# K loaded in rows of 16 KB with one batch and head per DMA engine, w2 in five chunks, the output stored in four transfers on two queues

## The chip, the cores and the metric

One core of a Trainium2 chip. The metric is the time of one execution on the device in microseconds (us), the median of several runs. A profile's span is some 1.8 us shorter than the time of the same run, because it begins with the first instruction and ends with the last; differences between spans and differences between times can be compared.

## The reference, cut to what matters

Four tokens (batch 4, one position each) go through a modulated layer norm, attention over cached keys and values, an output projection, a second layer norm and a feed-forward network with a ReLU.

```python
mod = (silu(c) @ w_mod)                       # six modulation vectors
h = layernorm(x) * (1 + ca) + sa
q = (h @ wq)                                  # 32 query heads of 128
k, v = k_cache[:, :, -1024:, :], v_cache[...] # 4 batches x 8 heads x 1024 keys x 128, bf16
o = softmax(q k^T / sqrt(128)) v
x = x + ga * (o @ wo)
h = layernorm(x) * (1 + cb) + sb
out = x + gb * (relu(h @ w1) @ w2)
```

K and V are 8 MB each, wq and wo 4 MB each, w_mod 3 MB, w1 and w2 1.8 MB each: 32 MB come in, 4 KB go out. Each of the 32 (batch, head) pairs has its 256 KB of K in one piece; two pairs start 1 MiB apart, because the cache holds 4,096 keys of which the last 1,024 are used.

## The kernel before

K comes in eight tiles of 1 MB, each half of the heads of one batch. A partition gets one row of 8 KB (32 keys). The order is "position, then head": 32 groups of four partitions, one partition for each of four heads.

```python
    def load_k(gi):
        b, par = gi // 2, gi % 2
        kt_ = kvpool.tile([P, NI, Dh], bf16, tag="kv", name=f"k{gi}")
        nc.sync.dma_start(
            out=kt_[:].rearrange("p j d -> p (j d)"),
            in_=k_src[b, par, :, S - W:, :].rearrange("h (p j) d -> p h (j d)", j=NI),
        )
        k_tiles.append(kt_)
```

TensorE transposes each tile in 32 blocks, VectorE and ScalarE move the result from PSUM to SBUF, and TensorE multiplies it with the queries. Softmax, the product with V, wo, w1 and w2 follow. All loads stand in one queue, issued by SyncE, in this order: K0, K1, w_mod, wq, K2 to K7, V, wo, w1, w2. w2 comes in chunks of 6, 5, 2 and 1 rows per partition so that little is left to do after the last; the result goes out in one transfer of 16 rows of 256 bytes:

```python
    W2_CHUNKS = [(0, 6), (6, 5), (11, 2), (13, 1)]
    ...
    nc.sync.dma_start(out=out.rearrange("b o (g n) -> (o g) b n", g=NH), in_=res[::BS, :])
```

Of the kernel before, what the change touches and what calls it, by code (L numbers as in the profile page):

```python
# [8 lines left out]
ACT = mybir.ActivationFunctionType  # L9
ALU = mybir.AluOpType  # L10
AX = mybir.AxisListType
bf16 = mybir.dt.bfloat16
f32 = mybir.dt.float32
i32 = mybir.dt.int32
# [3 lines left out]
def kernel(  # L18
# [14 lines left out]
    nc = tc.nc  # L33
    P = 128
    B, Sq, D = A_x.shape
    _, Hkv, S, Dh = A_k_cache.shape
    Hq = A_wq.shape[1] // Dh
    rep = Hq // Hkv
    W = min(4096, max(256, S // 4))
    Dff = B_w1.shape[1]  # L40
    DT = D // P
    FT = Dff // P
    KT = W // P
    assert Dh == P and B * Hq == P and Sq == 1
    CG = 32
    assert Hkv * rep == CG and B == 4 and rep == 4 and Hkv == 8 and DT == 4 and D == 512
    scale = float(Dh) ** -0.5
    EPS = 1e-5
    HALF = W // 2
    NHW = Hkv // 2  # L50
    NG = 2 * B
    KC = P // NHW
    NI = W // KC
    KAHEAD = 2
    NH = 4
    DH2 = D // NH
    BS = CG // B
# [3 lines left out]
    const = ctx.enter_context(tc.tile_pool(name="const", bufs=1))  # L61
    wts = ctx.enter_context(tc.tile_pool(name="wts", bufs=1))
    kvpool = ctx.enter_context(tc.tile_pool(name="kvpool", bufs=11))
    ktp = ctx.enter_context(tc.tile_pool(name="ktp", bufs=4))
    work = ctx.enter_context(tc.tile_pool(name="work", bufs=1))
    psA = ctx.enter_context(tc.tile_pool(name="psA", bufs=6, space=bass.MemoryType.PSUM))
# [7 lines left out]

    k_src = A_k_cache.rearrange("b (par hw) s d -> b par hw s d", par=2)
    k_tiles = []

    def load_k(gi):
        b, par = gi // 2, gi % 2
        kt_ = kvpool.tile([P, NI, Dh], bf16, tag="kv", name=f"k{gi}")  # L80
        nc.sync.dma_start(  # L81
            out=kt_[:].rearrange("p j d -> p (j d)"),
            in_=k_src[b, par, :, S - W:, :].rearrange("h (p j) d -> p h (j d)", j=NI),
        )
        k_tiles.append(kt_)

    for gi in range(KAHEAD):
        load_k(gi)
    wmod_sb = wts.tile([P, DT, 6 * D], bf16, tag="med", name="wmod_sb")
# [3 lines left out]
    for t in range(0, DT, 2):  # L93
        nc.sync.dma_start(out=wq_sb[:, t:t + 2, :], in_=wq_src[:, t:t + 2, :])
    for gi in range(KAHEAD, NG):
        load_k(gi)

    v_tiles = []
    for h in range(Hkv):
        vt_ = kvpool.tile([P, NI, Dh], bf16, tag="kv", name=f"v{h}")  # L100
        nc.sync.dma_start(
            out=vt_[:].rearrange("p j d -> p (j d)"),
            in_=A_v_cache[:, h, S - W:, :].rearrange("b (p j) d -> p b (j d)", j=NI),
        )
        v_tiles.append(vt_)
# [14 lines left out]

    W2_CHUNKS = [(0, 6), (6, 5), (11, 2), (13, 1)]
    assert sum(e for _, e in W2_CHUNKS) == FT
    w2_dst = w12[:, DT * Dff:DT * Dff + FT * D]
    for (m0, e) in W2_CHUNKS:
        nc.sync.dma_start(out=w2_dst[:, m0 * D:(m0 + e) * D],
                          in_=B_w2[m0 * P:(m0 + e) * P, :].rearrange("(q e) n -> q (e n)", e=e))
# [3 lines left out]
    ident_bf = const.tile([P, P], bf16, name="ident_bf")  # L130
    make_identity(nc, ident_bf[:])

    ident_k3 = const.tile([P, NHW, KC], bf16, name="ident_k")
    nc.gpsimd.memset(ident_k3[:], 0.0)
    nc.gpsimd.affine_select(out=ident_k3[:], in_=ident_k3[:], compare_op=ALU.not_equal, fill=1.0, base=0,
                            pattern=[[-1, NHW], [-NHW, KC]], channel_multiplier=1)
    ident_k = ident_k3[:].rearrange("p h k -> p (h k)")

# [17 lines left out]
                            base=0, pattern=[[-1, NL], [0, 2], [-NL, P // NL]], channel_multiplier=1)  # L156
# [19 lines left out]
    for t in range(DT):  # L176
# [8 lines left out]
                                   op0=ALU.is_ge, op1=ALU.max)  # L185
# [8 lines left out]
    sc_ps = psS.tile([P, W], f32, tag="s", name="sc_ps")  # L194
    IQ = NI // 4

    def k_transposes(gi):
        kT = ktp.tile([P, NI, NHW, KC], bf16, tag="kT", name=f"kT{gi}")
        for iq in range(4):
            tp = psA.tile([P, IQ, P], bf16, tag="t", name=f"ktp_{gi}_{iq}")  # L200
            for ii in range(IQ):
                nc.tensor.transpose(out=tp[:, ii, :], in_=k_tiles[gi][:, iq * IQ + ii, :], identity=ident_k)  # L202
            dst = kT[:, iq * IQ:(iq + 1) * IQ].rearrange("p i h k -> p i (h k)")
            if iq % 2 == 1:
                nc.vector.tensor_copy(out=dst, in_=tp[:])  # L205
            else:
                nc.scalar.copy(out=dst, in_=tp[:])  # L207
        return kT

    def k_scores(gi, kT):  # L210
        b, par = gi // 2, gi % 2
        for half in range(2):
            for hw in range(NHW):
                nc.tensor.matmul(  # L214
                    out=sc_ps[hw * CG:(hw + 1) * CG, half * HALF:(half + 1) * HALF],
                    lhsT=qpad[:, b, par, hw, :],
                    rhs=kT[:, half * (NI // 2):(half + 1) * (NI // 2), hw, :],
                    start=(gi == 0), stop=(gi == NG - 1),
                    tile_position=(0, hw * CG),
                )  # L220

    kts_pending = [k_transposes(gi) for gi in range(KAHEAD)]


    m4 = const.tile([P, B], f32, name="m4")
    nc.vector.tensor_reduce(out=m4[:], in_=ident_f[:].rearrange("p (hp b r) -> p b hp r", b=B, r=rep),
                            axis=AX.XY, op=ALU.add)
# [10 lines left out]
    for t in range(DT):  # L238
        nc.tensor.matmul(out=m5_ps[:], lhsT=siluT32[:, t, :], rhs=wmod_sb[:, t, 4 * D:5 * D],  # L239
                         start=(t == 0), stop=(t == DT - 1), tile_position=(0, 0))  # L240
# [68 lines left out]

    for gi in range(KAHEAD):  # L310
        k_scores(gi, kts_pending.pop(0))
    kts_pending.append(k_transposes(KAHEAD))
    for gi in range(KAHEAD, NG):
        if gi + 1 < NG:
            kts_pending.append(k_transposes(gi + 1))
        k_scores(gi, kts_pending.pop(0))



    mx = work.tile([P, 1], f32, name="mx")  # L320
    nc.vector.tensor_reduce(out=mx[:], in_=sc_ps[:], axis=AX.X, op=ALU.max)
    nb = work.tile([P, 1], f32, name="nb")
    nc.vector.tensor_scalar_mul(out=nb[:], in0=mx[:], scalar1=-scale)
    NQ = 4
# [4 lines left out]
    den4 = work.tile([P, NQ], f32, name="den4")  # L329
    p_rep = ktp.tile([P, NI // 2, P, 2], bf16, tag="kT", name="p_rep")  # L330
    p_w = p_rep[:].rearrange("q u c e -> q (u c e)").bitcast(i32).rearrange("q (w b) -> q w b", b=B)
    pT = ktp.tile([P, NI, P], bf16, tag="kT", name="pT")
    oT_ps = psA.tile([P, NHW, 2, B, rep], f32, tag="t", name="oT_ps")
# [9 lines left out]
    VEARLY = 3  # L343
    for iq in range(NQ):
        ws = slice(iq * WQ, (iq + 1) * WQ)
        nc.scalar.activation(out=e_sb[:, ws].rearrange("q (u k e) -> q u k e", k=KC, e=2),  # L346
                             in_=sc_ps[:, ws].rearrange("q (u e k) -> q u k e", e=2, k=KC), func=ACT.Exp,
                             bias=nb[:], scale=scale, accum_out=den4[:, iq:iq + 1])
    for iq in range(NQ):
# [123 lines left out]

    for (m0, m1) in [(0, 6), (6, FT)]:
        ffn1(m0, m1)
# [6 lines left out]
    nc.vector.tensor_tensor(out=res[:], in0=zg[:], in1=x12_ps[:], op=ALU.add)  # L482
    nc.sync.dma_start(out=out.rearrange("b o (g n) -> (o g) b n", g=NH), in_=res[::BS, :])

# [29 lines left out]
```

## Time and profile before

| | before |
|---|---|
| time, median (lowest to highest) | 85.94 us (85.81 to 85.98, 3 runs) |
| span of the profile | 84.1 us |
| bytes in | 31.99 MB |
| DMA engines busy | from 2 us to 80 us without a gap |
| TensorE busy | 57.5 us (68% of the span) |

Packet times in this document are medians over the trace's records of single DMA packets, and sums of them are what was recorded for all 16 engines, divided by 16. The kernel is bound by its loads, as the lines in the prediction show. Of the costliest groups of instructions one line is wanted later. Its columns: line, engine, operation, what is written and read, shapes, count; then busy us and mean ns of one; then idle time of the engine just before, and what ended it.

```profile
L202 PE MATMUL ktp<-ident_k,k 128*128 128x128 bf16 x256 | 18.4, 241 | 1.2 <-DMA k<-in_A_k_cache_dram 1.2
```

In the whole K stage TensorE waited only 1.2 us for K.

### The profile page before, as it was taken

What the parts mean: (1) busy time and instruction counts of PE and PEld (TensorE: products, weight loads), DVE (VectorE), ACT (ScalarE), POOL (GpSimd) and SP (SyncE); (2) the same over time, 40 slices, a digit from 0 to 9 for tenths busy, and PEclk for the clock granted to TensorE, in tenths of its full rate; (3) what the DMA queues carried; (4) which work ended last, traced back from release to release, by engine and by line L of the source; (5) the groups of instructions that cost most, each with busy time, mean ns of one, the idle gap of its engine ahead of it and who ended that gap; (6) DMA issues with size and microseconds to landing.
All of it is one profiled execution on the core that took longest, in us unless ns stands there. A gap on an engine that the chain in (4) does not pass through costs nothing.

```text
span 84.1 us, 2367 instructions
## 1 busy us (share of the span) xinstructions
PE 57.5 (68%) x1064; PEld 47.4 (56%) x1064; DVE 26.4 (31%) x73; ACT 23.5 (28%) x37; POOL 5.2 (6%) x20
## 2 busy tenths in 40 slices
PE   0029940499729899999999329996454478598840
PEld 0029940248629739977778029996452058588720
DVE  0144480030330103645665768500003020241420
ACT  2314670003020004977798196300000010001000
POOL 6980000000000000000000000000000000000000
PEclk9999999957955555999999995696555555555555
DMA  0999998999999999999999999999999999999500
GB/s 2 333 401 452 503 421 386 444 421 444 421 394 405 433 433 413 413 413 425 425 413 409 425 425 421 405 433 421 425 409 409 425 432 425 413 398 406 210 0 2
DMA packets 4077, 32.13 MB, mean 382 GB/s; under 512 B 476, under 2 KB 612, under 8 KB 996
## 3 DMA queue, kind: packets, MB, share of 16 engines
q1 hardware_dynamic: 4052, 31.99, 91.7%
q8 instruction: 8, 0.13, 0.6%
q10 hardware_dynamic: 16, 0.01, 0.0%
q14 instruction: 1, 0.01, 0.0%
HBM read 31.99 MB, written 0.00 MB: 381 GB/s over the span
## 4 chain that ended last, share of the span: by engine, by line
DMA 64%; PE 25%; DVE 3%; issue 2%; SPq 1%; ACT 1%; DVEq 0%
DMA w<-in_B_w_dram 24%; DMA v<-in_A_v_cache_dram 24%; DMA wmod_sb<-in_w_mod_dram 16%; PE ktp L202 9%; PE qT_ps L302 4%; PE sc_ps L214 4%; PE mT L253 2%; PE mT L255 2%; PE z_ps L470 2%; PE m_ps L236 2%; SPq L81 1%; PE m_ps L239 1%; PE gb_ps L244 1%; PE st_ps_var L269 1%; ACT lnv L286 0%
## 5 line engine op out<-in xcount | busy, mean ns | idle before, releaser
L202 PEld LDWEIGHTS <-k 128*128 128x128 bf16 x256 | 17.3, 110 | 3.9 <-issue 2.5
L202 PE MATMUL ktp<-ident_k,k 128*128 128x128 bf16 x256 | 18.4, 241 | 1.2 <-DMA k<-in_A_k_cache_dram 1.2
L207 ACT COPY kT<-ktp 128x1024 bf16<-128x1024 bf16 x16 | 15.5, 1016 | 13.2 <-PE ktp L202 12.1
L205 DVE COPY kT<-ktp 128x1024 bf16<-128x1024 bf16 x16 | 11.1, 691 | 11.6 <-PE ktp L202 11.3
L340 PE MATMUL oT_ps<-pT,v 128*128 128x16 bf16 x256 | 7.3, 172 | 2.5 <-issue 1.9
L340 PEld LDWEIGHTS <-v 128*128 128x128 bf16 x256 | 7.1, 100 | 2.7 <-issue 2.0
L214 PE MATMUL sc_ps<-kT,qpad 128*32 128x512 bf16 x64 | 5.6, 445 | 0.4 <-DVE qpad L306 0.4
L357 PE MATMUL pT_ps<-ident_bf,p_rep 128*128 128x128 bf16 x32 | 3.1, 278 | 2.9 <-DVE p_rep L351 2.9
L357 PEld LDWEIGHTS <-p_rep 128*128 128x128 bf16 x32 | 2.7, 127 | 3.4 <-DVE p_rep L351 3.4
L302 PE MATMUL qT_ps<-hT,wq_sb 128*128 128x4 bf16 x128 | 3.6, 166 | 1.4 <-DVE ab L295 1.4
L302 PEld LDWEIGHTS <-wq_sb 128*128 128x128 bf16 x128 | 3.5, 104 | 1.5 <-issue 1.5
L236 PE MATMUL m_ps<-wmod_sb,siluT 128*32 128x512 bf16 x16 | 1.3, 435 | 4.4 <-DMA wmod_sb<-in_w_mod_dram 4.4
L409 ACT COPY y<-y_ps 128x256 f32<-128x256 f32 x1 | 0.4, 372 | 11.4 <-DVE y L408 11.4
L404 PE MATMUL y_ps<-wo_sb,o 128*32 128x512 bf16 x16 | 2.1, 619 | 2.0 <-DMA wo_sb<-in_A_wo_dram 1.1
L177 PE MATMUL tp<-ident_bf,cx_sb 8*128 8x8 bf16 x4 | 0.3, 168 | 4.5 <-DMA cx_sb<-in_A_x_dram 4.5
L236 PEld LDWEIGHTS <-siluT 128*32 128x32 bf16 x16 | 0.4, 95 | 4.7 <-issue 4.5
L382 DVE TENSOR_TENSOR oT_sb<-oT_ps,rb 128x128 bf16<-128x128 f32 x1 | 0.3, 292 | 8.6 <-PE oT_ps L340 8.6
L416 PEld LDWEIGHTS <-wo_sb 128*128 128x128 bf16 x64 | 2.5, 121 | 0.6 <-DMA wo_sb<-in_A_wo_dram 0.6
L416 PE MATMUL y_ps<-o,wo_sb 128*128 128x4 bf16 x64 | 2.4, 173 | 0.5 <-DMA wo_sb<-in_A_wo_dram 0.5
L177 PEld LDWEIGHTS <-cx_sb 8*128 8x128 bf16 x4 | 0.2, 110 | 4.5 <-issue 4.5
L351 DVE TENSOR_TENSOR p_rep<-e_sb,mi 128x512 int32<-128x512 int32 x4 | 2.5, 685 | 0.7 <-ACT e_sb L346 0.7
L459 PE MATMUL u_ps<-ab,w 128*128 128x8 bf16 x56 | 2.4, 181 | 0.4 <-DMA w<-in_B_w_dram 0.4
(107 smaller groups left out, 57.0 us busy)
## 6 DMA issues: line engine op xcount, KB each, us to landing
k<-in_A_k_cache_dram SPq DMA_DIRECT2D x8, 1024.0 KB, 25.8
v<-in_A_v_cache_dram SPq DMA_DIRECT2D x8, 1024.0 KB, 19.9
wq_sb<-in_A_wq_dram SPq DMA_DIRECT2D x2, 2048.0 KB, 18.0
wo_sb<-in_A_wo_dram SPq DMA_DIRECT2D x4, 1024.0 KB, 19.9
wmod_sb<-in_w_mod_dram SPq DMA_DIRECT2D x1, 3072.0 KB, 13.7
w<-in_B_w_dram SPq DMA_DIRECT2D x1, 1792.0 KB, 21.7
w<-in_B_w_dram SPq DMA_DIRECT2D x1, 768.0 KB
w<-in_B_w_dram SPq DMA_DIRECT2D x1, 640.0 KB, 20.1
```

Of the source, the lines that this page charges most:

```text
L202: nc.tensor.transpose(out=tp[:, ii, :], in_=k_tiles[gi][:, iq * IQ + ii, :], identity=ident_k)
L205: nc.vector.tensor_copy(out=dst, in_=tp[:])
L207: nc.scalar.copy(out=dst, in_=tp[:])
L214: nc.tensor.matmul(out=sc_ps[hw * CG:(hw + 1) * CG, half * HALF:(half + 1) * HALF], lhsT=qpad[:, b, par, hw, :], rhs=kT[:, half * (NI // 2 ...
L236: nc.tensor.matmul(out=m4_ps[k * CG:(k + 1) * CG, :], lhsT=siluT32[:, t, :], rhs=wmod_sb[:, t, k * D:(k + 1) * D], start=(t == 0), stop=(t ...
L302: nc.tensor.matmul(out=qT_v[:, hq, :], lhsT=wq_sb[:, t, hq * Dh:(hq + 1) * Dh], rhs=hT[:, t, :], start=(t == 0 and hq == 0), stop=(t == DT ...
L340: nc.tensor.matmul(out=oT_ps[:, hw, par].rearrange("p b r -> p (b r)"), lhsT=v_tiles[h][:, i, :], rhs=pT[:, i, c0:c0 + B * rep], start=(fi ...
L351: nc.vector.tensor_tensor(out=p_w[:, ws, :], in0=e_w[:, ws].unsqueeze(2).to_broadcast([P, WQ // 2, B]), in1=mi4[:].unsqueeze(1).to_broadca ...
L357: nc.tensor.transpose(out=tp[:, ii, :], in_=p_rep[:, i // 2, :, i % 2], identity=ident_bf[:])
L404: nc.tensor.matmul(out=y4_ps[q0:q0 + CG, :], lhsT=o4[:, l, g % 2, g // 2, :], rhs=wo_sb[:, g, l, :], start=(g == 0 and l < 4), stop=(g == ...
L416: nc.tensor.matmul(out=y_ps[:, m, :], lhsT=wo_sb[:, g, l, m::DT], rhs=o4[:, l, g % 2, g // 2, 0:B], start=False, stop=(g == NP - 1 and l = ...
L459: nc.tensor.matmul(out=u_ps[:, m - m0].rearrange("p s b -> p (s b)"), lhsT=w1_cols(t, m), rhs=ab[:, t].rearrange("p s b -> p (s b)"), star ...
```

## The change

Three things at once. K comes in 2 MB tiles: each partition gets 16 KB (64 keys) instead of 8, and the order is "pair of batch and head, then position", so that 16 groups of 8 partitions arise, meant to give each of the 16 DMA engines one pair and one piece of 128 KB in HBM. w2 comes in five chunks. The store is cut in four, two on each of two queues.

```diff
-    k_src = A_k_cache.rearrange("b (par hw) s d -> b par hw s d", par=2)
+    k_src = A_k_cache.rearrange("b h s d -> (b h) s d")
...
+    def load_k(ti, parts):
+        bh, kh = ti // 2, ti % 2
+        kt_ = kvpool.tile([P, NI8, Dh], bf16, tag="kv", name=f"k{ti}")
+        e = NI8 // parts
+        s0 = S - W + kh * WH
+        src = k_src[bh * NQK:(bh + 1) * NQK, s0:s0 + WH, :].rearrange("q (k j) d -> q k (j d)", j=NI8)
+        for i0 in range(0, NI8, e):
+            nc.sync.dma_start(out=kt_[:, i0:i0 + e, :].rearrange("p j d -> p (j d)"), in_=src[:, :, i0 * Dh:(i0 + e) * Dh])
...
-    W2_CHUNKS = [(0, 6), (6, 5), (11, 2), (13, 1)]
+    W2_CHUNKS = [(0, 4), (4, 4), (8, 3), (11, 2), (13, 1)]
...
-    for (m0, m1) in [(0, 6), (6, FT)]:
+    for (m0, m1) in [(0, 8), (8, FT)]:
...
-    nc.sync.dma_start(out=out.rearrange("b o (g n) -> (o g) b n", g=NH), in_=res[::BS, :])
+    out_g = out.rearrange("b o (g n) -> g (b o) n", g=NH)
+    for g in range(NH):
+        eng = nc.sync if g % 2 == 0 else nc.scalar
+        eng.dma_start(out=out_g[g], in_=res[g * CG:(g + 1) * CG:BS, :])
```

Cut away: the K and V buffers become five of 16 KB per partition instead of eleven of 8 KB; transposes, score matmuls and exponentials follow the new order of keys; the maximum before the exponential is taken in two halves. The source of a K transfer, as it stands in the program, has these dimensions (elements of 2 bytes; step and count, slowest first):

```
before   [4096, 32] [524288, 4] [1, 4096]     32 groups of 4 partitions
changed  [524288, 16] [8192, 8] [1, 8192]     16 groups of 8 partitions
```

More of the change, by code (lines that the diff above doesn't have):

```diff
@@ L50 @@
     NHW = Hkv // 2
-    NG = 2 * B
     KC = P // NHW
     NI = W // KC
-    KAHEAD = 2
+    NQK = 16
+    KC8 = P // NQK
+    NI8 = 2 * NI
+    WH = KC8 * NI8
+    NT = B * Hkv * W // (NQK * WH)
+    assert NQK == 2 * Hkv and WH == HALF and NT == 4
     NH = 4
@@ L62 @@
     wts = ctx.enter_context(tc.tile_pool(name="wts", bufs=1))
-    kvpool = ctx.enter_context(tc.tile_pool(name="kvpool", bufs=11))
-    ktp = ctx.enter_context(tc.tile_pool(name="ktp", bufs=4))
+    kvpool = ctx.enter_context(tc.tile_pool(name="kvpool", bufs=5))
+    ktp = ctx.enter_context(tc.tile_pool(name="ktp", bufs=2))
     work = ctx.enter_context(tc.tile_pool(name="work", bufs=1))
@@ L72 @@
     nc.scalar.dma_start(out=cx_sb[B:2 * B, :], in_=A_x.rearrange("b o d -> (b o) d"))
-    k_src = A_k_cache.rearrange("b (par hw) s d -> b par hw s d", par=2)
+    k_src = A_k_cache.rearrange("b h s d -> (b h) s d")
     k_tiles = []
-    def load_k(gi):
-        b, par = gi // 2, gi % 2
-        kt_ = kvpool.tile([P, NI, Dh], bf16, tag="kv", name=f"k{gi}")
-        nc.sync.dma_start(
-            out=kt_[:].rearrange("p j d -> p (j d)"),
-            in_=k_src[b, par, :, S - W:, :].rearrange("h (p j) d -> p h (j d)", j=NI),
-        )
+    def load_k(ti, parts):
[6 more added lines that the diff above has]
+            nc.sync.dma_start(out=kt_[:, i0:i0 + e, :].rearrange("p j d -> p (j d)"), in_=src[:, :, i0 * Dh:(i0 + e) * Dh])
         k_tiles.append(kt_)
-    for gi in range(KAHEAD):
-        load_k(gi)
+    load_k(0, 1)
     wmod_sb = wts.tile([P, DT, 6 * D], bf16, tag="med", name="wmod_sb")
@@ L94 @@
         nc.sync.dma_start(out=wq_sb[:, t:t + 2, :], in_=wq_src[:, t:t + 2, :])
-    for gi in range(KAHEAD, NG):
-        load_k(gi)
+    for ti in range(1, NT):
+        load_k(ti, 1 if ti + 1 < NT else 2)
     v_tiles = []
     for h in range(Hkv):
-        vt_ = kvpool.tile([P, NI, Dh], bf16, tag="kv", name=f"v{h}")
+        if h % 2 == 0:
+            v2_ = kvpool.tile([P, 2, NI, Dh], bf16, tag="kv", name=f"v{h}")
+        vt_ = v2_[:, h % 2]
         nc.sync.dma_start(
-            out=vt_[:].rearrange("p j d -> p (j d)"),
+            out=vt_.rearrange("p j d -> p (j d)"),
             in_=A_v_cache[:, h, S - W:, :].rearrange("b (p j) d -> p b (j d)", j=NI),
@@ L131 @@
     make_identity(nc, ident_bf[:])
-    ident_k3 = const.tile([P, NHW, KC], bf16, name="ident_k")
-    nc.gpsimd.memset(ident_k3[:], 0.0)
-    nc.gpsimd.affine_select(out=ident_k3[:], in_=ident_k3[:], compare_op=ALU.not_equal, fill=1.0, base=0,
-                            pattern=[[-1, NHW], [-NHW, KC]], channel_multiplier=1)
-    ident_k = ident_k3[:].rearrange("p h k -> p (h k)")
     siluT32 = const.tile([P, DT, CG], bf16, name="siluT32")
@@ L195, with k_transposes, k_scores @@
     IQ = NI // 4
-    def k_transposes(gi):
-        kT = ktp.tile([P, NI, NHW, KC], bf16, tag="kT", name=f"kT{gi}")
+    kTs = {}
+    def k_transposes(ti, sh):
+        if sh == 0:
+            kTs[ti] = ktp.tile([P, NI8, P], bf16, tag="kT", name=f"kT{ti}")
         for iq in range(4):
-            tp = psA.tile([P, IQ, P], bf16, tag="t", name=f"ktp_{gi}_{iq}")
+            tp = psA.tile([P, IQ, P], bf16, tag="t", name=f"ktp_{ti}_{sh}_{iq}")
+            i0 = sh * NI + iq * IQ
             for ii in range(IQ):
-                nc.tensor.transpose(out=tp[:, ii, :], in_=k_tiles[gi][:, iq * IQ + ii, :], identity=ident_k)
-            dst = kT[:, iq * IQ:(iq + 1) * IQ].rearrange("p i h k -> p i (h k)")
+                nc.tensor.transpose(out=tp[:, ii, :], in_=k_tiles[ti][:, i0 + ii, :], identity=ident_bf[:])
             if iq % 2 == 1:
-                nc.vector.tensor_copy(out=dst, in_=tp[:])
+                nc.vector.tensor_copy(out=kTs[ti][:, i0:i0 + IQ, :], in_=tp[:])
             else:
-                nc.scalar.copy(out=dst, in_=tp[:])
-        return kT
-    def k_scores(gi, kT):
-        b, par = gi // 2, gi % 2
-        for half in range(2):
-            for hw in range(NHW):
+                nc.scalar.copy(out=kTs[ti][:, i0:i0 + IQ, :], in_=tp[:])
+    def k_scores(ti, i0=0, i1=NI8):
+        bh, kh = ti // 2, ti % 2
+        for bl in range(2):
+            for h in range(Hkv):
+                b, par, hw = 2 * bh + bl, h // NHW, h % NHW
+                p0 = bl * (P // 2) + h * KC8
                 nc.tensor.matmul(
-                    out=sc_ps[hw * CG:(hw + 1) * CG, half * HALF:(half + 1) * HALF],
+                    out=sc_ps[hw * CG:(hw + 1) * CG, kh * WH + i0 * KC8:kh * WH + i1 * KC8],
                     lhsT=qpad[:, b, par, hw, :],
-                    rhs=kT[:, half * (NI // 2):(half + 1) * (NI // 2), hw, :],
-                    start=(gi == 0), stop=(gi == NG - 1),
+                    rhs=kTs[ti][:, i0:i1, p0:p0 + KC8],
+                    start=(b == 0 and par == 0), stop=(b == B - 1 and par == 1 and i1 == NI8),
                     tile_position=(0, hw * CG),
                 )
-    kts_pending = [k_transposes(gi) for gi in range(KAHEAD)]
+    for sh in range(2):
+        k_transposes(0, sh)
     m4 = const.tile([P, B], f32, name="m4")
@@ L308 @@
             in_=qT_ps[:, par].rearrange("p h r b -> p b h r"))
-    for gi in range(KAHEAD):
-        k_scores(gi, kts_pending.pop(0))
-    kts_pending.append(k_transposes(KAHEAD))
-    for gi in range(KAHEAD, NG):
-        if gi + 1 < NG:
-            kts_pending.append(k_transposes(gi + 1))
-        k_scores(gi, kts_pending.pop(0))
-    mx = work.tile([P, 1], f32, name="mx")
-    nc.vector.tensor_reduce(out=mx[:], in_=sc_ps[:], axis=AX.X, op=ALU.max)
+    k_scores(0)
+    for sh in range(2):
+        k_transposes(1, sh)
+    k_transposes(2, 0)
+    k_scores(1)
+    k_transposes(2, 1)
+    k_transposes(3, 0)
+    k_scores(2)
+    mx2 = work.tile([P, 2], f32, name="mx2")
+    nc.vector.tensor_reduce(out=mx2[:, 0:1], in_=sc_ps[:, 0:WH], axis=AX.X, op=ALU.max)
+    k_transposes(3, 1)
+    k_scores(3, 0, NI)
+    k_scores(3, NI, NI8)
+    nc.vector.tensor_reduce(out=mx2[:, 1:2], in_=sc_ps[:, WH:W], axis=AX.X, op=ALU.max)
     nb = work.tile([P, 1], f32, name="nb")
-    nc.vector.tensor_scalar_mul(out=nb[:], in0=mx[:], scalar1=-scale)
+    nc.vector.tensor_scalar(out=nb[:], in0=mx2[:, 0:1], scalar1=mx2[:, 1:2], scalar2=-scale, op0=ALU.max, op1=ALU.mult)
     NQ = 4
@@ L329 @@
     den4 = work.tile([P, NQ], f32, name="den4")
-    p_rep = ktp.tile([P, NI // 2, P, 2], bf16, tag="kT", name="p_rep")
-    p_w = p_rep[:].rearrange("q u c e -> q (u c e)").bitcast(i32).rearrange("q (w b) -> q w b", b=B)
-    pT = ktp.tile([P, NI, P], bf16, tag="kT", name="pT")
+    p_full = ktp.tile([P, NI8, P], bf16, tag="kT", name="p_full")
+    p_rep = p_full[:, 0:NI, :].rearrange("q n c -> q (n c)").rearrange("q (u c e) -> q u c e", c=P, e=2)
+    p_w = p_rep.rearrange("q u c e -> q (u c e)").bitcast(i32).rearrange("q (w b) -> q w b", b=B)
+    pT = ktp.tile([P, NI8, P], bf16, tag="kT", name="pT")
     oT_ps = psA.tile([P, NHW, 2, B, rep], f32, tag="t", name="oT_ps")
@@ L343 @@
     VEARLY = 3
-    for iq in range(NQ):
-        ws = slice(iq * WQ, (iq + 1) * WQ)
-        nc.scalar.activation(out=e_sb[:, ws].rearrange("q (u k e) -> q u k e", k=KC, e=2),
-                             in_=sc_ps[:, ws].rearrange("q (u e k) -> q u k e", e=2, k=KC), func=ACT.Exp,
-                             bias=nb[:], scale=scale, accum_out=den4[:, iq:iq + 1])
+    e_v = e_sb[:].rearrange("q (u a k s e) -> q a s u k e", a=2, k=KC8, s=2, e=2)
+    for kh in range(2):
+        for sh in range(2):
+            c0 = kh * WH + sh * NI * KC8
+            nc.scalar.activation(out=e_v[:, kh, sh],
+                                 in_=sc_ps[:, c0:c0 + NI * KC8].rearrange("q (u e k) -> q u k e", e=2, k=KC8), func=ACT.Exp,
+                                 bias=nb[:], scale=scale, accum_out=den4[:, 2 * kh + sh:2 * kh + sh + 1])
     for iq in range(NQ):
```

## The prediction

> **What bounds the kernel now.** I read the strip of the span first, then the chain that ended last, then the tail of the timeline. The strip says whether any stage leaves the DMA engines idle:
>
> ```profile
> DMA  0999998999999999999999999999999999999500
> GB/s 2 333 401 452 503 421 386 444 421 444 421 394 405 433 433 413 413 413 425 425 413 409 425 425 421 405 433 421 425 409 409 425 432 425 413 398 406 210 0 2
> ...
> q1 hardware_dynamic: 4052, 31.99, 91.7%
> ```
>
> The first row is the busy share in tenths of the 16 DMA engines in 40 slices of 2.1 us, the second what they moved, the third the load queue: packets, MB, share of the 16 engines' span. From slice 1 to slice 36 the engines are full. 31.99 MB has to come in, and nothing leaves the chip but 4 KB. The chain of waits says the same in time:
>
> ```profile
> 31.13 4.91 PE ktp L202 x64
> ...
> 39.39 19.88 DMA v<-in_A_v_cache_dram
> 59.28 20.14 DMA w<-in_B_w_dram
> 79.42 0.04 issue
> 79.46 1.31 PE z_ps L470 x30
> 80.79 0.30 DVE zg L480
> 81.12 0.29 DVE res L482
> ```
>
> Columns: start, length (us), what. TensorE is on the chain only up to 39 us, and only because a transfer issued then stands 20 us deep in a queue that is full anyway. From there to 79.4 it is V, then the weights. That TensorE is not the limit later shows in where it waits for V:
>
> ```profile
> 60.06 1.07 PE L340 MATMUL oT_ps<-pT,v 128*128 128x16 bf16 x34 [1.87 <-issue]
> ...
> 61.77 1.02 PE L340 MATMUL oT_ps<-pT,v 128*128 128x16 bf16 x32 [0.63 <-DMA v<-in_A_v_cache_dram]
> ...
> 66.73 1.05 PE L404 MATMUL y_ps<-wo_sb,o 128*32 128x512 bf16 x8 [1.15 <-DMA wo_sb<-in_A_wo_dram]
> ...
> 81.44 0.69 SPq L483 DMA_DIRECT2D out_dram<-res  x1
> ```
>
> The brackets are idle time before the group. TensorE stands idle 1.87 + 0.63 = 2.5 us just before the last V tile, so everything earlier in the K stage and the softmax has about 2.5 us of slack before it could move the end.
>
> Three numbers come from the trace's records of single packets and completions. **Packets:** on the load queue, medians are 312 ns for 8,192 bytes, 611 for 16,384, 199 for 5,120, 236 for 6,144, 84 for 2,048, 46 for 1,024, with hardly any spread (the 90th percentile of the 8,192-byte ones is 319). A DMA engine therefore works at its own rate, and the row length counts: two 8,192-byte rows take 624 ns, one of 16,384 takes 611, so a row costs about 13 ns beyond its bytes. **Full engines:** each engine handles 8 rows of every load; 160 rows of 8 KB, 16 of 16 KB, 8 of 24 KB, 8 of 14 KB and the four chunks of w2 sum to 49.92 + 9.78 + 7.30 + 4.30 + 4.52 = 75.8 us, against 76.3 us from the first packet (2.18) to the first engine's finish (78.53). There is no gap to win. **The last engine:** the 16 completions of the last w2 chunk run from 78.53 to 80.41 us. About half of the engines lag, by up to 1.9 us, each after one of eight 16 KB packets on the instruction queue, which take 1.02 to 1.11 us and cost the engine that carries one some 1.1 to 1.5 us. The end is 80.41 plus a fixed tail: last four matmuls, two VectorE steps, store, closing barrier, to 84.08 (3.67 us).
>
> [...]
>
> **The change, part by part.**
>
> K rows. Before: 8 transfers, 64 rows of 8 KB per engine, 64 x 312 = 19.97 us. After: three transfers of 2 MB with 16 KB rows and a fourth in two halves of 8 KB rows, so per engine 24 x 611 + 16 x 312 = 19.66 us. Gain 0.31 us, on the path, as the engines are full.
>
> w2 in five chunks of 4, 4, 3, 2, 1 rows instead of 6, 5, 2, 1. A row of 4,096 bytes should take 161 ns and one of 3,072 bytes 122 (estimates, on the line through 84 and 199 ns). Per engine 8 x (161 + 161 + 122 + 84 + 46) = 4.59 us against 8 x (236 + 199 + 84 + 46) = 4.52. Loss 0.07 us, on the path. What it could buy, earlier starts for the second feed-forward product, is hidden: the matmuls that matter are those after the last chunk, which has one row before and after.
>
> Loads go from 28 to 26, two completion packets of 9 ns less per engine: 0.02 us. The last landing moves by -0.31 + 0.07 - 0.02 = -0.26 us, to about 80.15.
>
> Store. Before: one transfer of 16 rows of 256 bytes; issue starts at 81.44 and takes 0.69, packets run at 82.73, the last completion is at 83.14. After: SyncE and ScalarE each issue two transfers of four rows. The nearest thing in the trace are the two 4-row loads that ScalarE issues at the start: issue 0.55 and 0.26 us, the first packet 0.92 us after the issue of the first began. Two in a row take 0.55 to 0.85 us per issuer, side by side, so the last store leaves between 0.14 earlier and 0.16 later[...]. I take -0.05 us.
>
> TensorE. The same 256 transposes and 32 evictions. The score matmuls go from 64 of 512 columns to 48 of 512 and 32 of 256: the same columns, 16 more instructions. The first K tile is 2 MB, so its transposes begin near 8.4 us instead of 6.0; they need 5.5 us and still end before w_mod lands (15.8). The second K tile lands whole at about 31.8 (where its second half lands now), so its transposes start about 0.8 us later than the 31.06 of now. Then the stage runs at TensorE's pace, as now: six half tiles at 1.96 us of transposes plus about 3.4 us of scores, 15.2 us, to about 47.0, where it ends at 46.98 today. The maximum in two halves takes about half of the 1.22 us off what follows. All of it is before the 2.5 us of slack: nothing at the end.
>
> Buffers. Five buffers of 16 KB per partition instead of eleven of 8 KB. The third V pair waits for the second K tile's transposes (about 36.8 us), when some 6 MB are still queued ahead, 14 us of work at 420 GB/s. No gap.
>
> Sum: -0.26 - 0.05 = -0.3 us of 85.94, that is 85.6.
>
> **The rivals.** *Streams collide in HBM.* If 16 engines at a pitch of 1 MiB are slowed, the K rows stretch beyond 611 ns. [...] For it: a pattern that the kernel has not had. [...] *The slow engine decides.* The end is set by the engine that carried an instruction block. Sixteen more score matmuls, 32 instructions of some 2,000, shift the blocks in time; if a block lands on an engine that has already lost 1.1 us, or a ninth is fetched before 80 us, the end moves out by about 1.1 us and eats the gain: 86.7. Against it: in the trace eight blocks hit different engines, and the last one started as late as 78.25. If the blocks fell more kindly, a few tenths would be won. *The score stage becomes the bound.* Two-megabyte tiles make the hand-over coarser[...]. It would have to lose 2.5 us to be seen. *The store costs more.* Four issues with four completions to wait for: +0.3 us at worst, as the issues are serial in pairs.
>
> **Range and chances.** The sum of the sure terms is a third of a microsecond; the instruction blocks and the store can each move it by a few tenths either way, and the HBM pitch only upward. Hence 85.6, with 85.1 to 86.3 as the range. A win of over 2% would need 1.7 us, and no part has that to give, since the same bytes pass through engines that are full: 2%. A loss of over 2% needs the HBM pitch or a badly placed block: 5%. Within 2%: 93%.
>
> **What would show it.** Right: the median 16,384-byte packet of the K loads at 611 ns; DMA full to slice 36; the last completion of w2 near 80.15 us; TensorE still idle before the last V tile; issue of the last store to its packets no longer than 1.3 us. Wrong: K packets over 640 ns; idle tenths in the DMA row between slices 10 and 30; no idle time before the last V tile; a spread of the last completions well over 1.9 us.

Passages that no trace or run of this case shows are cut from this text, where the marks stand: a paragraph of general statements, the two sizes of the first rival with the argument against it, and a clause each on the start of the store and the pace of the scores. The forecast's sum: -0.31 + 0.07 - 0.02 = -0.26 us for the last landing and -0.05 for the store, together -0.3 of 85.94, that is 85.6. The -0.05 is an estimate within the range from 0.14 earlier to 0.16 later.

## The result

| | before | changed |
|---|---|---|
| time, median (lowest to highest) | 85.93 us (85.81 to 85.98, 4 runs) | 106.73 us (106.15 to 107.31, 4 runs) |
| span | 84.1 us | 105.2 us |
| K packets per engine, sum | 20.52 us | 29.28 (16,384 bytes) + 9.38 (8,192 bytes) = 38.65 us |
| K packets, median | 312 ns (8,192 bytes) | 1,259 ns (16,384 bytes), 599 ns (8,192 bytes) |
| wq packets, median | 611 ns | 613 ns |
| last load landed | 80.41 us | 100.54 us |
| from there to the end | 3.67 us | 4.67 us |

The ratio is 1.2425, 95% interval 1.2369 to 1.2482.

The strip of the page after, same rows and columns as before (a slice is now 2.6 us):

```profile
DMA  4899899999999999999999999999999999999500
GB/s 89 188 224 230 227 439 439 414 411 417 442 287 212 218 206 206 212 218 202 224 234 218 262 364 417 417 417 430 414 414 417 420 417 418 427 403 407 210 1 2
...
q1 hardware_dynamic: 3760, 31.99, 92.1%
```

The row of busy tenths looks the same as before: full. Only the row below tells. In slices 1 to 4 (the first K tile) and 12 to 21 (the other three) the engines move 188 to 234 GB/s, about half of the 400 to 440 that they move for w_mod, wq, V and the weights. So a 9 in the busy row stood here for 224 GB/s (slice 2) as well as for 439 (slice 5). The chain of waits (start, length, what):

```profile
0.73 12.92 DMA k<-in_A_k_cache_dram
...
13.67 48.48 DMA k<-in_A_k_cache_dram
...
64.40 19.86 DMA wo_sb<-in_A_wo_dram
84.28 15.94 DMA w<-in_B_w_dram
100.22 0.04 issue
100.26 0.65 PE z_ps L484 x12
100.91 0.02 issue
100.93 0.30 DVE zg L494
101.23 0.02 issue
101.26 0.29 DVE res L496
```

K now makes up the chain to 62 us; the second piece runs from the issue of the last K tile to its landing, so w_mod and wq, queued before it, pass in it too. The group of transposes shows it from TensorE's side, 14.9 us of waiting where there was 1.2:

```profile
L205 PE MATMUL ktp<-ident_bf,k 128*128 128x128 bf16 x256 | 21.5, 265 | 15.0 <-DMA k<-in_A_k_cache_dram 14.9
```

And the end of the timeline, the store (start, length of both issues, queue):

```profile
101.57 1.55 SPq L500 DMA_DIRECT2D out_dram<-res  x2
101.58 1.30 ACTq L500 DMA_DIRECT2D out_dram<-res  x2
```

One issue took 0.69 us before; now each queue needs two, of 0.60 to 0.76 us each, one behind the other. That is the added 1.0 us after the last landing.

### The profile page after: what moved, and what is told of

It reads as the page before. It is cut to its first block, busy times and chain, and to the rows that moved or that the text cites. A ratio compares the mean times of both kernels' runs of the same rounds, so it can differ in the third digit from the quotient of the medians.

```text
span 105.2 us, 2395 instructions
## 1 busy us (share of the span) xinstructions
PE 59.7 (57%) x1080; PEld 50.9 (48%) x1080; DVE 26.1 (25%) x74; ACT 23.8 (23%) x37; POOL 4.8 (5%) x18
## 4 chain that ended last, share of the span: by engine, by line
DMA 92%; another core or an unknown queue 2%; PE 1%; DVE 1%; SPq 1%; issue 0%
DMA k<-in_A_k_cache_dram 58%; DMA wo_sb<-in_A_wo_dram 19%; DMA w<-in_B_w_dram 15%; PE z_ps L484 1%; SPq L107 1%; DVE zg L494 0%; DVE res L496 0%
## 5 line engine op out<-in xcount | busy, mean ns | idle before, releaser
L205 PE MATMUL ktp<-ident_bf,k 128*128 128x128 bf16 x256 | 21.5, 265 | 15.0 <-DMA k<-in_A_k_cache_dram 14.9
L205 PEld LDWEIGHTS <-k 128*128 128x128 bf16 x256 | 20.6, 124 | 17.1 <-DMA k<-in_A_k_cache_dram 16.7
L217 PE MATMUL sc_ps<-kT,qpad 128*32 128x512 bf16 (+1 forms) x80 | 5.2, 388 | 0.6 <-DVE qpad L310 0.4
L371 PE MATMUL pT_ps<-ident_bf,p_full 128*128 128x128 bf16 x32 | 3.3, 296 | 3.8 <-DVE p_full L365 3.8
L371 PEld LDWEIGHTS <-p_full 128*128 128x128 bf16 x32 | 3.0, 137 | 4.2 <-DVE p_full L365 4.1
L365 DVE TENSOR_TENSOR p_full<-e_sb,mi 128x512 int32<-128x512 int32 x4 | 2.5, 686 | 2.1 <-ACT e_sb L360 2.1
L217 PEld LDWEIGHTS <-qpad 128*32 128x32 bf16 x80 | 1.9, 102 | 2.2 <-DVE kT L207 0.5
L484 PE MATMUL z_ps<-w,uT 128*32 128x128 bf16 x56 | 2.2, 303 | 0.7 <-DMA w<-in_B_w_dram 0.5
L373 ACT COPY pT<-pT_ps 128x1024 bf16<-128x1024 bf16 x2 | 2.0, 1012 | 2.3 <-PE pT_ps L371 2.3
```

Of the source, the lines that this page charges most:

```text
L205: nc.tensor.transpose(out=tp[:, ii, :], in_=k_tiles[ti][:, i0 + ii, :], identity=ident_bf[:])
L217: nc.tensor.matmul(out=sc_ps[hw * CG:(hw + 1) * CG, kh * WH + i0 * KC8:kh * WH + i1 * KC8], lhsT=qpad[:, b, par, hw, :], rhs=kTs[ti][:, i0 ...
L365: nc.vector.tensor_tensor(out=p_w[:, ws, :], in0=e_w[:, ws].unsqueeze(2).to_broadcast([P, WQ // 2, B]), in1=mi4[:].unsqueeze(1).to_broadca ...
L371: nc.tensor.transpose(out=tp[:, ii, :], in_=p_rep[:, i // 2, :, i % 2], identity=ident_bf[:])
L373: nc.scalar.copy(out=pT[:, iq * IQ:(iq + 1) * IQ, :], in_=tp[:])
L484: nc.tensor.matmul(out=z_ps[nh * CG:(nh + 1) * CG, :], lhsT=uT32[:, m, :], rhs=w2_sb[:, m, nh * DH2:(nh + 1) * DH2], start=(m == 0), stop= ...
```

## The experiments

**Three theories for the K rate.** A: sixteen streams that start 1 MiB apart collide in HBM (the first rival of the prediction). B: which partitions are written together sets the rate, wherever the rows lie in HBM, and 16 groups of 8 do worse than 32 of 4. (The records also gave a mechanism for B. No trace or run of this case shows it; it is cut from them where the marks stand, with the theories C and F, which rest on it.) The third theory, that 16 KB rows as such are slow, falls at once: wq has such rows and takes 613 ns in the same trace, and the last K tile with its 8 KB rows is doubled too (599 against 312 ns).

### e1: another pitch in HBM

```diff
-        src = k_src[bh * NQK:(bh + 1) * NQK, s0:s0 + WH, :].rearrange("q (k j) d -> q k (j d)", j=NI8)
+        PITCH = S * Dh + 2048
+        q0 = bh * (NQK - 1)
+        src = k_flat[s0 * Dh + q0 * PITCH:s0 * Dh + (q0 + NQK) * PITCH].rearrange("(q x) -> q x", x=PITCH)
+        src = src[:, 0:WH * Dh].rearrange("q (k x) -> q k x", k=KC8)
```

> The changed kernel, but its 16 groups of K rows start 1 MiB + 4 KiB apart in HBM instead of 1 MiB (other addresses, so a wrong result on purpose; shapes, row length, grouping and everything else as in the changed kernel). Theory A (streams a power of two apart collide in HBM): the K packets of 16,384 bytes fall back from about 1,130 to about 611 ns and the time to about 87 us (85.93 - 0.26 for the packets + 1.0 for the store). Theory B[...]: the HBM addresses do not matter, packets stay near 1,130 ns and the time near 106.7 us.

(The "1,130 ns" in these texts is the median over all 16 KB packets, wq among them; the K packets alone have 1,259.)

### e2: 32 groups of 4 partitions, still 1 MiB apart

```diff
-        s0 = S - W + kh * WH
-        src = k_src[bh * NQK:(bh + 1) * NQK, s0:s0 + WH, :].rearrange("q (k j) d -> q k (j d)", j=NI8)
+        s0 = S - W + ti * (W // 4)
+        src = k_src[:, s0:s0 + W // 4, :].rearrange("q (k j) d -> q k (j d)", j=NI8)
```

> The changed kernel, but each K transfer takes 4 rows of 16 KB from each of all 32 (batch, head) pairs instead of 8 rows from each of 16 (wrong result on purpose, the rest of the program does not know of it). Starts are still 1 MiB apart in HBM, but the slowest dimension of the source is 32 groups of 4 partitions. Theory A (pitch in HBM): nothing gained, packets near 1,130 ns, time near 106.7 us. Theory B[...]: packets back at 611 ns, time about 87 us.

### e3: 16 groups of 8 partitions, close together in HBM

```diff
-        src = k_src[bh * NQK:(bh + 1) * NQK, s0:s0 + WH, :].rearrange("q (k j) d -> q k (j d)", j=NI8)
+        src = k_src[ti * Hkv:(ti + 1) * Hkv, S - W:S, :].rearrange("h (p j) d -> p h (j d)", j=NI8)
```

> The changed kernel, but each K transfer is one batch, with the position in the sequence as the slowest dimension of the source: 16 groups that start 16 KB apart in HBM, each of 8 rows of 16 KB, one from each head (wrong result on purpose). Groups of 8 partitions as in the changed kernel, but neighbouring engines read neighbouring addresses. Theory A (pitch in HBM): the rate comes back, packets 611 ns, time about 87 us. Theory B (groups of 8 partitions): packets stay near 1,130 ns and the time near 106.7 us.

| run | groups | starts in HBM | K packets of 16,384 bytes, median | time |
|---|---|---|---|---|
| changed kernel | 16 x 8 | 1 MiB apart | 1,259 ns | 106.73 us |
| e1 | 16 x 8 | 1 MiB + 4 KiB apart | 1,246 ns | 106.73 us (2 runs) |
| e3 | 16 x 8 | 16 KB apart | 1,272 ns | 106.85 us (2 runs) |
| e2 | 32 x 4 | 1 MiB apart | 611 ns | 87.27 us (2 runs) |

The GB/s rows of e1, e2 and e3 (their slices are 2.6, 2.1 and 2.6 us):

```profile
GB/s 77 214 231 213 256 422 431 422 413 444 419 275 213 238 200 213 231 206 206 225 241 235 278 400 419 416 419 425 425 422 410 422 410 417 444 388 396 147 1 2
```

```profile
GB/s 2 324 399 456 437 449 399 422 422 437 414 437 414 453 406 452 372 430 422 407 426 422 410 414 422 430 422 422 410 422 418 414 431 435 390 395 328 76 0 1
```

```profile
GB/s 52 252 206 219 225 450 450 375 463 413 419 300 200 244 200 225 200 231 188 241 213 244 247 394 428 406 416 435 413 422 413 419 416 421 443 385 403 192 1 2
```

Only e2 has no valley. The addresses in HBM do not matter in either direction; the cut into groups is everything. Theory A is out, for these pitches. e2 also shows how much of the loss this is: with the K loads right and all else as in the change, 19.5 of the 20.8 us are gone.

All three results passed the comparison with the reference although K came from wrong places. Why the comparison does not see K was not looked into; "correct" says nothing about K in this case, in the changed kernel and in e8 either.

### e6, e9, e12: the partitions by themselves

Theory B speaks of partitions, and e1 to e3 show only groups. So I wrote small kernels with nothing but loads, one after the other, told apart by row size. After two loads to all 128 partitions (e6), each load goes to sixteen partitions (eight in e9) that lie a fixed step apart, meant to give each engine a single partition for all its rows.

```python
    def single(step, nbytes):          # e6; e9 has 8 partitions and 16 rows, e12 has 16 and 16
        e = nbytes // 2
        src = k_rows[0:16, 0:NR * 8192].rearrange("q (k x) -> q k x", x=8192)[:, :, 0:e]
        nc.sync.dma_start(out=few[0:15 * step + 1:step, :, 0:e], in_=src)
```

> A kernel of its own (output wrong on purpose): eight loads, one after the other, each read from 1 MiB pitches of K and told apart by its row size. First 128 partitions as 32 groups of 4 (16,384 bytes), then as 16 groups of 8 (14,336 bytes), then six loads in which each of 16 engines writes 8 rows into one partition only, the 16 partitions lying 8, 7, 6, 4, 2 and 1 apart (7,680, 7,168, 6,656, 6,144, 5,632 and 5,120 bytes). Theory B[...]: packets at 611 ns for the first; doubled (about 1,070 against 538) for the second; for steps 8, 4 and 2 [...]all packets doubled (about 585, 472 and 436);[...] for step 1 [...]packets at about 800. Rival B2 (16 groups are slow[...], for instance in how the transfer is cut up): steps 7 and 6 look like step 8, all packets doubled, and step 1 like step 2. Rival A (pitch in HBM, all loads have it): no difference between the loads.

> A kernel of its own (output wrong on purpose): six loads, one after the other, each by eight DMA engines, each engine writing 16 rows into one partition.[...] Steady packets (after the first few of each engine) against a free packet of the size. Load 1, partitions 0, 4 .. 28 (8,192 bytes, free 312 ns)[...]. Load 2, 0, 5 .. 35 (7,680, free 293)[...]. Load 3, 0, 8 .. 56 (7,168, free 275)[...]. Load 4, 0 to 7 (6,656, free 256)[...]. Load 5, 1, 10 .. 64 (6,144, free 237)[...]. Load 6, 64, 68 .. 92 (5,632, free 218)[...]. Theory B[...]: loads 1, 5 and 6 free; load 2 three quarters of the packets free, a quarter doubled; load 3 doubled; load 4 fourfold.[...] Theory D ([...]the slow engines hold back all the others): load 2 all doubled, loads 1, 5 and 6 free.

> A kernel of its own (output wrong on purpose): five loads, one after the other, each by all sixteen DMA engines, each engine writing 16 rows into one partition. It asks why, in e6_ports, the loads with steps 7 and 6 were doubled throughout[...]. Free packets are 312, 293, 275, 256 and 237 ns. Load 1, partitions 32, 36 .. 92 (8,192 bytes)[...]. Load 2, 11, 18 .. 116 (7,680)[...]. Load 3, 28, 32 .. 88 (7,168)[...]. Load 4, 0, 7 .. 105 (6,656): [...]as in e6_ports. Load 5, 0, 8 .. 120 (6,144)[...]. Theory B[...]: loads 1 and 2 free, load 3 free for 14 of 16 engines,[...] load 5 doubled. Theory E[...]: loads 1 and 2 free, loads 3, 4 and 5 doubled throughout.[...]

Each ran once (state unknown); packets of one run are compared with each other only. The trace does not name the engine of a packet: that an engine keeps to one partition is assumption. The table counts the second half of each load, to leave its start out. "Free" is within 1.3 of the free time, "double" 1.6 to 2.6 times, "fourfold" over 3 times.

```
run  partitions             free  double  fourfold  of
e6   128 as 32 x 4            64      0       0      64
e6   128 as 16 x 8             0     64       0      64
e6   0, 8 .. 120               0     64       0      64
e6   0, 7 .. 105               1     60       0      64
e6   0, 6 .. 90                0     64       0      64
e6   0, 4 .. 60                0     62       0      64
e6   0, 2 .. 30                1     61       0      64
e6   0, 1 .. 15                0      0      64      64
e9   0, 4 .. 28               63      0       0      64
e9   0, 5 .. 35               45     19       0      64
e9   0, 8 .. 56                0     64       0      64
e9   0, 1 .. 7                 0      0      64      64
e9   1, 10 .. 64              64      0       0      64
e9   64, 68 .. 92             64      0       0      64
e12  32, 36 .. 92            128      0       0     128
e12  11, 18 .. 116           128      0       0     128
e12  28, 32 .. 88            109     19       0     128
e12  0, 7 .. 105               0    127       0     128
e12  0, 8 .. 120               0    128       0     128
```

Which partitions are written together decides. In e12 alone, with sixteen partitions and 16 rows to each in every load, step 7 from partition 11 is free and step 7 from partition 0 is doubled (511 against 256 ns). Step 4 is free from partition 32 (e12) and doubled from partition 0 (e6). All these loads read rows from the same 16 places in HBM. Eight partitions are free, doubled or fourfold as well (e9). Only partitions one apart are fourfold (3.8 times the free time), sixteen of them (e6) and eight (e9). With 28, 32 .. 88 only some packets are slow, and just two of the sixteen completions come late (at 60.7 and 61.0 us, the others by 57.6). Rival B2, that 16 groups are slow as such, falls with e6's step 1, which is fourfold where step 2 is doubled, and with the first two loads of e12, which are free. Theory D falls with the second load of e9, where 45 of 64 packets are free.

In sixteen of the nineteen loads the outcome is the one recorded for theory B. Three do not fit: steps 7 and 6 from partition 0 with sixteen partitions are doubled throughout (547 against 275 ns for step 7 in e6), though B had expected a slowing of some packets only. e12 repeated step 7 with the same outcome, so it is no accident. Theory E expected it, but of 28, 32 .. 88 too, where 109 of 128 packets are free. It stays open, and so does what it is in a set of partitions that slows it: these runs show which sets are slow, not why. It does not touch the K loads, whose cut into 16 groups of 8 the second load of e6 repeats (64 of 64 doubled).

### e10 and e11: the K part alone

```diff
-    W2_CHUNKS = [(0, 4), (4, 4), (8, 3), (11, 2), (13, 1)]
+    W2_CHUNKS = [(0, 6), (6, 5), (11, 2), (13, 1)]
...
-    for (m0, m1) in [(0, 8), (8, FT)]:
+    for (m0, m1) in [(0, 6), (6, FT)]:
...
-    out_g = out.rearrange("b o (g n) -> g (b o) n", g=NH)
-    for g in range(NH):
...
+    nc.sync.dma_start(out=out.rearrange("b o (g n) -> (o g) b n", g=NH), in_=res[::BS, :])
```

(e11: with the source of e2 besides.)

> The changed kernel with the store and w2 of the kernel before, so the K part of the change alone (16 groups of 8 partitions). If the parts add up: 106.73 - 1.18 for the store - 0.01 for w2 = about 105.5 us.

> The same, but with the K loads as 32 groups of 4 partitions (wrong K data on purpose, the rest of the K part as in the change). If the grouping is the whole of the loss and the store costs 1.18 us: 87.27 - 1.18 = about 86.1 us, so that 16 KB rows win nothing. If the coarser tiles now bind the compute side, over 86.5 us.

e10: 105.27 us (105.04 to 105.67, 4 runs), before 86.02 in the same rounds, ratio 1.2247 (1.2214 to 1.2279). The K part alone costs 19.25 us; its packets sum to 29.1 + 9.2 = 38.4 us per engine against 20.5, which is 17.9 of it.

e11: 86.36 us (86.33 to 86.43, 4 runs), ratio 1.0044 (1.0027 to 1.006), between the two outcomes expected. So even with the loads right, the longer rows win nothing and the K part costs 0.34 us. The loads still end the kernel: the last one lands at 80.76 us instead of 80.41, and the last four matmuls, one for each quarter of the columns, start 0.04 us after it in both traces. Their weight loads in the timelines, of e11 and of the kernel before:

```profile
80.80 0.11 PEld L485 LDWEIGHTS <-uT 128*32 128x32 bf16 x3
```

```profile
80.45 0.10 PEld L470 LDWEIGHTS <-uT 128*32 128x32 bf16 x3
```

The first of the 16 engines finishes at 78.55 us, as before (78.53), but the last one lags it by 2.20 us instead of 1.88. The compute side has come close behind the loads, as the chain of waits shows:

```profile
31.91 7.96 PE ktp L206 x96
39.87 0.98 PE sc_ps L218 x16
...
56.20 3.27 PE oT_ps L352 x128
59.47 0.32 PE rb_ps L393 x2
59.79 1.13 PE oT_ps L352 x46
60.93 1.82 issue
62.74 2.37 PE oT_ps L352 x82
```

From 31.9 us on the chain follows TensorE and what hangs on it: the product with V ends at 65.1 us, where it ended at 62.8 in the kernel before. The waits for wo, w1 and w2 that followed there (1.15 + 0.48 + 0.39 + 0.30 = 2.3 us) had room for about that much. So the coarser tiles made the compute side late and used up its slack, but the 0.34 us are those of the last landing.

### e4, e5, e7: the store and w2

e4 is the kernel before with the store of the change, e5 with its w2, e7 with the store in two transfers of 8 rows, one per queue:

```diff
+    out_g = out.rearrange("b o (g n) -> g b (o n)", g=NH)
+    nc.sync.dma_start(out=out_g[0:2], in_=res[0:2 * CG:BS, :])
+    nc.scalar.dma_start(out=out_g[2:4], in_=res[2 * CG:4 * CG:BS, :])
```

> The kernel before with the store alone changed: four transfers on two queues. In the changed kernel each of the four issues took 0.60 to 0.76 us and the last completion came 1.0 us later after the last arithmetic than before. If that is the store's own cost: 85.93 + 1.0 = about 86.9 us. If it belonged to the slowed kernel: about 85.9 us, as the prediction had it.

> The kernel before with w2 alone changed: five chunks and the first feed-forward product split 8 and 6. By packet times +0.07 us, by the completions of the changed kernels +0.1 us: about 86.0 us. Rival: the smaller chunks let the second product start earlier and win a few tenths, 85.6 us.

> The kernel before with the store cut into two transfers of 8 rows, one on each queue. If the store's cost is two issues of some 0.7 us one behind the other on each queue, two issues side by side cost nothing: about 85.9 us. If two queues that issue at the same time slow each other, or each transfer more costs at the end, about 86.3 us or more.

| | time | before, same rounds | ratio (95%) |
|---|---|---|---|
| e4, store in four | 87.11 us (4 runs) | 85.93 | 1.0137 (1.0121 to 1.0154) |
| e7, store in two | 86.09 us (5 runs) | 85.93 | 1.0018 (1.0006 to 1.003) |
| e5, w2 in five chunks | 85.94 us (5 runs) | 85.93 | 1.0004 (0.9992 to 1.0016) |

The issues at the end of the timelines of e4 and of e7:

```profile
81.46 1.49 SPq L486 DMA_DIRECT2D out_dram<-res  x2
81.47 1.33 ACTq L486 DMA_DIRECT2D out_dram<-res  x2
```

```profile
81.52 0.66 SPq L484 DMA_DIRECT2D out_dram<-res  x1
81.53 0.59 ACTq L485 DMA_DIRECT2D out_dram<-res  x1
```

An issue costs 0.6 to 0.75 us whether it carries 16, 8 or 4 rows, at this place. Side by side on two queues they overlap; one behind the other on a queue they add up. The store in four costs 1.18 us, w2 nothing that can be seen. The second issue makes 0.80 of the 1.18 (1.49 us against 0.69); the rest was not taken apart.

### e8: the 16 KB rows done right

The K loads of e2 with scores and exponentials rewritten for 4 rows from each of 32 pairs (128 score matmuls of 256 columns, eight exponentials of 128 columns instead of four of 256), and the old store and w2:

```diff
-    NQK = 16
+    NQK = 32
...
-        src = k_src[bh * NQK:(bh + 1) * NQK, s0:s0 + WH, :].rearrange("q (k j) d -> q k (j d)", j=NI8)
+        src = k_src[:, s0:s0 + WH, :].rearrange("q (k j) d -> q k (j d)", j=NI8)
...
+    e_v = e_sb[:].rearrange("q (u t k s e) -> q t s u k e", t=NT, k=KC8, s=2, e=2)
```

> K in rows of 16 KB as in the change, but 4 rows from each of all 32 (batch, head) pairs per transfer, with the scores, the exponentials and their order rewritten to suit, so a right result; store and w2 as in the kernel before. If the groups of 8 partitions are the whole cause of the loss: no loss left, and of the 0.31 us that I had worked out for the longer rows something between 0 and 0.3, so 85.6 to 85.9 us. If the coarser tiles or the score matmuls of 256 columns cost something that the slow loads hid so far: over 86.5 us.

89.27 us (88.75 to 90.53, 6 runs, one of them slow), ratio 1.0388 (1.036 to 1.0417): slower than before by 3.3 us. (Its profile has a span of 86.7 us for a run of 89.26, 2.5 us less and not 1.8; some 0.7 of the 3.3 us lie outside the trace.) Its loads end at 80.67 us; the last matmuls start only at 82.88, so here the compute side ends last. From its chain of waits:

```profile
50.15 2.90 ACT e_sb L357 x16
...
57.42 3.31 PE oT_ps L348 x128
60.73 1.05 issue
...
65.60 2.38 issue
67.98 0.24 PE oT_ps L348 x2
```

The eight exponentials with their read-outs took 2.9 us, where the four of e11 took 1.9. The idle times marked "issue" are the more telling lines: 1.05 and 2.38 us, where e11 has one of 1.82. The second lies between two matmuls of the product with V at 65.6 us, and the last V tile had landed at 62.0, so it was not waiting for data. No kernel here beats the one before.

## Why the prediction was wrong

**The load rate of K: this step failed, and decided the result.** The prediction took 24 x 611 + 16 x 312 ns per engine from packets of the same size in other loads. Measured: 38.65 us instead of 19.66. The packet time of a size held here only for some sets of partitions written together: 16,384 bytes took 611 ns in 32 groups of 4 (e2) and 1,259 ns in 16 groups of 8, and the small loads were free, doubled or fourfold by the partitions alone. All loads in the load queue of the kernel before have 32 or more groups in their slowest dimension, so nothing in its trace could show another time; the small spread that I took as proof of "its own rate" was the spread of one good pattern. What the change altered, and what I read past, was the slowest dimension, from 32 to 16. The prediction took 16 streams, one per engine, as harmless but for their addresses. Its own sign of being wrong, K packets over 640 ns, came true.

**The rival "streams collide in HBM"** had the right place, but the wrong mechanism: e1 and e3 move the streams and change nothing (1,246 and 1,272 against 1,259 ns), e2 leaves them 1 MiB apart and is fast (611 ns). The 5% for "slower" was therefore too little for a pattern that the kernel had never had, and for a second reason that was not on the list at all.

**The store** was put at -0.05 us and measured at +1.18 (e4). The mis-sized term is the issue: I took 0.55 and 0.26 us from two 4-row loads at the start, where the second issue is short. At the end each of the four took 0.60 to 0.76 us, so two in a row need 1.3 to 1.55 us where one needed 0.69. The "+0.3 us at worst" named the right cause, the serial pairs, with a quarter of its size. (The last completion of the old store is at 83.19 us, not 83.14; that changes nothing.)

**w2**: +0.07 us predicted, 0.01 measured with an interval of about 0.1 us either side (e5). Nothing speaks against it: the rows of 4,096 and 3,072 bytes took 161 and 124 ns, where 161 and 122 had been estimated.

**The slack.** I counted 1.87 + 0.63 us of idle before the last V tile as slack. Only the 0.63, which names V as its releaser, was waiting for data. The 1.87 is marked "issue", waiting for nothing that the profile shows, and it belongs to a place in the program: it comes after 190 of the 256 matmuls of the product with V, in the middle of a V tile, in the four traces whose TensorE program is the old one up to there (before, e4, e5, e7), and after 174 in the six with the changed one (changed, e1, e2, e3, e10, e11), which has 16 score matmuls more. In e8, with 64 more, there are two such gaps, after 128 and after 254, with 128 matmuls and their 128 weight loads between them. In these eleven traces the gaps last 1.0 to 2.4 us, and each ends 2.3 to 2.6 us after the start of a 16 KB packet, itself 1.0 to 1.4 us long, on the queue that the page calls instruction. What TensorE waits for there the traces do not show; no run was made to test it.

The conclusion drawn from the slack, nothing at the end, holds in e11 all the same, with some luck: its product with V is 2.3 us late, and the loads still end the kernel. In e8 it does not hold. The K stage was to end at 47.0 us, and in e11 the scores end at 48.8. The term that was mis-sized is the transposes: 1.96 us per half tile was their pace at a granted clock of 1.00 (kernel before, 36.5 to 45.8 us), and in e11 the first three took 7.96 us. Between 31.9 and 36.0 us the granted clock was 0.50 there, and 0.78 in the kernel before.

In the changed kernel itself all this is hidden by the slow loads:

```profile
79.05 1.50 PE L351 MATMUL oT_ps<-pT,v 128*128 128x16 bf16 x50 [1.62 <-issue]
81.83 1.02 PE L351 MATMUL oT_ps<-pT,v 128*128 128x16 bf16 x32 [1.27 <-DMA v<-in_A_v_cache_dram]
```

TensorE does wait for the last V tile there, as foretold, but after loads that were themselves late.

**The 0.31 us from longer rows** did not come to the end even with the packets at 611 ns. In e11 the median packet is 611 ns, as foretold, but the K packets of an engine sum to 20.44 us against 20.52 before, a gain of 0.08: the medians (64 x 312 ns = 19.97 us) leave out the longer packets. **The slow engine** rival took more than that back. The completions of the last chunk spread over 1.85 to 1.92 us in the four traces without the K part and over 2.16 to 2.71 us in the seven with it. That the instruction packets do this, of which again eight were fetched in the changed kernel, was not tested.

The parts add up. K alone 19.25 (e10), store 1.18 (e4), w2 0.01 (e5) make 20.44 of the measured 20.80 us; the parts come from other rounds than the whole, whose own times spread over 1.2 us.

## What to carry to other kernels

Before a load's shape is changed, write down how its slowest dimension cuts the 128 partitions, and measure a cut that the kernel has not had. Loads to all 128 partitions with a slowest dimension of 32 or 128 ran here at full rate (611 ns in e2, 613 for wq), those with 16 groups of 8 at half (1,259 ns), with the busy row at 8 or 9 in both; sixteen partitions at 32, 36 .. 92 were free too (e12), so it is not the number 16. The busy row does not tell the cases apart: look at GB/s or at packet times. And count as slack only idle time that names a releaser; a small transfer at the very end cost its issue here (0.69 us), so two on one queue cost two (1.49 us in e4).
